# A fused attention and FFN kernel: a planner in the kernel fixes one issue order for all engines, and the opening goes by query tiles

## The chip, the cores and the metric

The kernel runs on one core of a Trainium2 chip. Times are device microseconds (us) of that core, medians over several executions. The "span" is the time from the first to the last instruction of the one execution that the profile shows; the device time is 1.7 to 1.9 us more than the span (2.7 in one run). A core has a matrix engine (TensorE, PE in the profile, with PEld for its weight loads), VectorE (DVE), ScalarE (ACT), GpSimd (POOL) and a sync engine (SP). GpSimd and the sync engine only issue DMAs here, apart from a little set-up. Each engine works through its own list of instructions in order; semaphores make it wait for the others.

## The reference, cut to what matters

```python
# q, k, v: (4 batches, 8 heads, 768 rows, 64) float32
scores = (q @ k.T) / 8 + bias            # bias falls with distance, one slope per head
scores = where(keep, scores, -1e9)       # keep: the last 96 rows, and the first 8 ("global") ones
a = exp(scores - max);  a = a / sum(a)
x = (a @ v) as (3072, 512)               # heads side by side
h = maximum(x @ w_in, 0)                 # w_in  (512, 2048)
out = (h * h) @ w_out                    # w_out (2048, 512)
```

As a row looks back at most 95 rows, a tile of 128 queries needs two blocks of keys: its own tile and the one before ("before" blocks, in which the first rows are replaced by the global ones: `kb` and `vb` are the copies of k and v made so).

## The kernel before

Work goes by eight half batches of 384 rows (three tiles of 128), numbered 0 to 7. While TensorE does the FFN of one half batch, the attention of the next is mixed in. In the names of the profile: `trp` are the transposes of q and k, `sp` the scores, `ex` and `phat` the exponentials and the weighted ones, `av` the product with v, `tm` the normalised result, `trx` its transposes and `xt` the FFN input; `hps`, `hr` and `h` belong to the first FFN layer, `yps` and `y` to the second. Only TensorE's order is fixed by hand; the framework orders the other engines.

```python
def score(b, half, a, g):                # twice per head pair a: g = 0, 1
    ...
    sp = ps_big.tile([P, 2, 512], FP32, name="sp", tag="big")     # 3 buffers of 2 PSUM banks
    for i, (r, before) in enumerate(blocks):                      # 2 or 3 blocks
        for e in range(2):                                        # two heads, 64 rows each
            nc.tensor.matmul(sp[:, e, i * P:(i + 1) * P], lhsT=..., rhs=..., start=True, stop=True)
    nc.scalar.activation(out=ex[:, :, 0:n], in_=sp[:, :, 0:n], func=AF.Exp, scale=scale)
    nc.vector.tensor_tensor(out=phat[:, :, c0:c0 + n], in0=ex[:, :, 0:n], in1=mask[...], op=ALU.mult)

def attention(hb):                       # the list of side jobs
    jobs = [lambda: fix_v(b, half)]      # the vb copies on VectorE
    for a in range(NPAIR + 3):           # prep, score 0, score 1, attend, to_x, staggered
        ...

fill_index()
for h0 in range(0, H, 4):
    load(0, 0, h0, h0 + 4)               # 18 DMAs of four heads each, all on GpSimd
fill_masks()
for c in range(4): load_w_in(c)
load(0, 1, 0, H)
for c in range(4): load_w_out(c)
load(1, 0, 0, H)
with tc.manual_schedule(engines={PE}):
    for job in attention(0): job()
    for hb in range(NHB):
        if 1 <= hb and hb + 2 < NHB: load((hb + 2) // 2, hb % 2, 0, H)
        main = ffn(hb)                   # 16 jobs of the first layer, 12 of the second
        side = attention(hb + 1) if hb + 1 < NHB else []
        for job in merge(main, side, 1, len(main) - 4): job()
```

The softmax here doesn't subtract the row's maximum and nothing guards it: scores larger than these inputs give would overflow.

Of the kernel before, what the change touches and what calls it, by code (L numbers as in the profile page):

```python
# [8 lines left out]
FP32 = mybir.dt.float32  # L9
# [3 lines left out]
PE = mybir.EngineType.PE  # L13

P = 128


def merge(main, side, start, stop):

    out = []  # L20
    done = 0
    for i, f in enumerate(main):
        if i >= start:
            want = len(side) if i >= stop else (i - start) * len(side) // (stop - start)
            while done < want:
                out.append(side[done])
                done += 1
        out.append(f)
    return out + side[done:]
# [3 lines left out]
def kernel(  # L33
# [23 lines left out]
    GR = 32  # L57
    scale = 1.0 / math.sqrt(D)
    slopes = [2.0 ** (-8.0 * (h + 1) / H) for h in range(H)]

# [6 lines left out]
    phat_p = ctx.enter_context(tc.tile_pool(name="phat", bufs=3))  # L67
    tm_p = ctx.enter_context(tc.tile_pool(name="tm", bufs=3))
    h_p = ctx.enter_context(tc.tile_pool(name="hp", bufs=2))
    y_p = ctx.enter_context(tc.tile_pool(name="yp", bufs=2))  # L70
    ps_big = ctx.enter_context(tc.tile_pool(name="ps_big", bufs=3, space=bass.MemoryType.PSUM))
    ps_att = ctx.enter_context(tc.tile_pool(name="ps_att", bufs=2, space=bass.MemoryType.PSUM))


    dist = const.tile([P, 2 * P], FP32, name="dist")
    distc = const.tile([P, 2 * P], FP32, name="distc")
    pidx = const.tile([P, 1], FP32, name="pidx")
    ident = const.tile([P, P], FP16, name="ident")
    local = const.tile([P, 2 * P], FP16, name="local")
    ge0 = const.tile([P, 2 * P], FP16, name="ge0")  # L80
    isg = const.tile([P, 1], FP32, name="isg")
    far = const.tile([P, 2 * P], FP16, name="far")
    decay = const.tile([P, H, 2 * P], FP16, name="decay")
    gw = const.tile([P, H, 2 * P], FP16, name="gw")
    cg = const.tile([P, H], FP16, name="cg")

    mask = const.tile([P, H, 5 * P], FP16, name="mask")
# [3 lines left out]
    def fill_index():  # L91
        nc.gpsimd.iota(dist, pattern=[[1, 2 * P]], base=0, channel_multiplier=-1,
                       allow_small_or_imprecise_dtypes=True)
        nc.gpsimd.iota(pidx, pattern=[[0, 1]], base=0, channel_multiplier=1,
                       allow_small_or_imprecise_dtypes=True)
        nc.vector.tensor_scalar(out=ident, in0=dist[:, 0:P], scalar1=0.0, scalar2=None,
                                op0=ALU.is_equal)

    def fill_masks():
        nc.vector.tensor_scalar(out=distc, in0=dist, scalar1=0.0, scalar2=None, op0=ALU.max)  # L100
        for h in range(H):
            nc.scalar.activation(out=decay[:, h, :], in_=distc, func=AF.Exp, scale=-slopes[h])
            nc.vector.memset(cg[:, h:h + 1], math.exp(-slopes[h] * NL))
        nc.vector.tensor_scalar(out=ge0, in0=dist, scalar1=0.0, scalar2=None, op0=ALU.is_ge)
        nc.vector.scalar_tensor_tensor(out=local, in0=dist, scalar=float(NL), in1=ge0,
                                       op0=ALU.is_lt, op1=ALU.mult)
        nc.vector.tensor_scalar(out=isg, in0=pidx, scalar1=float(NG), scalar2=None,
                                op0=ALU.is_lt)
        nc.vector.tensor_scalar(out=far, in0=local, scalar1=0.5, scalar2=isg,
                                op0=ALU.is_lt, op1=ALU.mult)  # L110
        nc.vector.tensor_tensor(out=gw, in0=far[:, None, :].to_broadcast([P, H, 2 * P]),
                                in1=cg[:, :, None].to_broadcast([P, H, 2 * P]), op=ALU.mult)
        own, bef = slice(0, P), slice(P, 2 * P)
        nc.vector.tensor_tensor(out=mask[:, :, P:3 * P], in0=decay,
                                in1=local[:, None, :].to_broadcast([P, H, 2 * P]), op=ALU.mult)
        nc.vector.tensor_tensor(out=mask[:, :, 0:P], in0=mask[:, :, P:2 * P],
                                in1=gw[:, :, own], op=ALU.add)
        nc.vector.tensor_tensor(out=mask[:, :, 2 * P:3 * P], in0=mask[:, :, 2 * P:3 * P],
                                in1=gw[:, :, bef], op=ALU.add)
        nc.vector.tensor_copy(out=mask[:, :, 3 * P:5 * P], in_=mask[:, :, P:3 * P])  # L120


# [3 lines left out]
    batches = []  # L126
    for b in range(B):
        bt = Batch()
        bt.sq = [None, None]
        bt.sk = [None, None]  # L130
        batches.append(bt)

    def load(b, half, h0, h1):
        bt = batches[b]
        if half == 0 and h0 == 0:
            bt.qk = qk_p.tile([P, 2, NPAIR, S], FP16, name="qk", tag="qk")
            bt.kb = qk_p.tile([P, NPAIR, NT - 1, P], FP16, name="kb", tag="kb")
            bt.v = qk_p.tile([P, NT, H, D + 1], FP16, name="v", tag="v")
            bt.vb = qk_p.tile([P, NT - 1, H, D + 1], FP16, name="vb", tag="vb")
            nc.vector.memset(bt.v[:, :, :, D:D + 1], 1.0)  # L140
        if h0 == 0:
            bt.sq[half] = stage_p.tile([P, HT, H, D], FP16, name="sq", tag="sq")
            bt.sk[half] = stage_p.tile([P, HT, H, D], FP16, name="sk", tag="sk")
        rows = slice(half * HALF, (half + 1) * HALF)
        for src, dst in ((q, bt.sq[half]), (k, bt.sk[half]),
                         (v, bt.v[:, half * HT:(half + 1) * HT, :, 0:D])):
            for t in range(HT):
                r0 = half * HALF + t * P
                nc.gpsimd.dma_start(  # L149
                    out=dst[:, t, h0:h1, :],  # L150
                    in_=src[b, h0:h1, r0:r0 + P, :].rearrange("h p d -> p h d"))

    def fix_v(b, half):
        bt = batches[b]
        t0, t1 = (0, HT) if half == 0 else (HT, NT - 1)
        nc.vector.tensor_copy(out=bt.vb[GR:GR * 2, t0:t1], in_=bt.v[GR:GR * 2, t0:t1])
        nc.vector.tensor_copy(out=bt.vb[2 * GR:P, t0:t1], in_=bt.v[2 * GR:P, t0:t1])  # L157
        for t in range(t0, t1):
            nc.vector.tensor_copy(out=bt.vb[0:GR, t], in_=bt.v[0:GR, 0])

    def prep(b, half, a):
        bt = batches[b]
        trp = ps_att.tile([P, 2, HT, P], FP16, name="trp", tag="att")
        for i, st in enumerate((bt.sq[half], bt.sk[half])):
            for t in range(HT):
                nc.tensor.transpose(out=trp[:, i, t, :], in_=st[:, t, 2 * a:2 * a + 2, :],  # L166
                                    identity=ident)
        nc.scalar.copy(out=bt.qk[:, :, a, half * HALF:(half + 1) * HALF],  # L168
                       in_=trp.rearrange("p i t c -> p i (t c)"))
        kt = bt.qk[:, 1, a, :].rearrange("p (t c) -> p t c", c=P)  # L170
        t0, t1 = (0, HT) if half == 0 else (HT, NT - 1)
        nc.vector.tensor_copy(out=bt.kb[:, a, t0:t1, GR:P], in_=kt[:, t0:t1, GR:P])  # L172
        nc.vector.tensor_copy(out=bt.kb[:, a, t0:t1, 0:GR],  # L173
                              in_=kt[:, 0:1, 0:GR].to_broadcast([P, t1 - t0, GR]))


    GROUPS = {
        0: ([(0, 0), (1, 0), (1, 1)], [(2, 0), (2, 1)]),
        1: ([(3, 0), (3, 1), (4, 0)], [(4, 1), (5, 0), (5, 1)]),
    }  # L180
    MASK0 = {0: (0, 1), 1: (1, 2)}
    phats = {}
    tms = {}
    xts = {}

    def score(b, half, a, g):
        bt = batches[b]
        if g == 0:
            phats[b, half, a] = phat_p.tile([P, 2, 6 * P], FP16, name="phat", tag="phat")
        phat = phats[b, half, a]  # L190
        blocks = GROUPS[half][g]
        n = len(blocks) * P
        c0 = 3 * P * g
        m0 = MASK0[half][g] * P
        sp = ps_big.tile([P, 2, 512], FP32, name="sp", tag="big")
        for i, (r, before) in enumerate(blocks):
            for e in range(2):
                rows = slice(e * D, (e + 1) * D)
                lhsT = (bt.kb[rows, a, r - 1, :] if before
                        else bt.qk[rows, 1, a, r * P:(r + 1) * P])  # L200
                nc.tensor.matmul(sp[:, e, i * P:(i + 1) * P], lhsT=lhsT,  # L201
                                 rhs=bt.qk[rows, 0, a, r * P:(r + 1) * P],
                                 start=True, stop=True)
        ex = phat_p.tile([P, 2, 3 * P], FP16, name="ex", tag="ex")
        nc.scalar.activation(out=ex[:, :, 0:n], in_=sp[:, :, 0:n], func=AF.Exp, scale=scale)  # L205
        nc.vector.tensor_tensor(out=phat[:, :, c0:c0 + n], in0=ex[:, :, 0:n],  # L206
                                in1=mask[:, 2 * a:2 * a + 2, m0:m0 + n], op=ALU.mult)
# [161 lines left out]
```

## Time and profile before

The time before was 261.35 us as the median of three runs (261.56 with a fourth).

| TensorE, kernel before | us |
|---|---|
| first FFN matmul | 27.0 |
| first layers of half batches 1 to 7 begin | 67.15, 94.43, 121.96, 151.53, 179.05, 206.06, 233.58 |
| last matmul ends / span | 254.5 / 258.2 |

The head of the page, and the rows for TensorE and its clock in 40 equal slices of the span (6.5 us each; a digit is tenths):

```profile
span 258.2 us, 4590 instructions
...
PE 227.6 (88%) x1888; PEld 125.0 (48%) x1888; DVE 139.6 (54%) x331; ACT 135.0 (52%) x201; POOL 75.9 (29%) x95
...
PEclk9999999985999999999999999999999999999999
```

TensorE is busy most of the time, but its clock falls in the ninth and tenth slice (52 to 65 us). The timeline of TensorE shows why. Columns: start in us, us, engine, line, operation, output and inputs, shape, count, and in brackets the idle time before it with what ended it.

```profile
32.94 0.23 PE L166 MATMUL trp<-ident,sk 128*128 128x128 f16 x1 [0.65 <-DMA sk<-in_k_dram]
33.84 0.23 PE L166 MATMUL trp<-ident,sk 128*128 128x128 f16 x1 [0.67 <-DMA sk<-in_k_dram]
...
35.76 0.81 PE L272 MATMUL hps<-xt,w_in_sb 128*128 128x384 f16 x4
36.50 0.23 PE L201 MATMUL sp<-qk 64*128 64x128 f16 x2
36.57 0.22 PE L201 MATMUL sp<-qk,kb 64*128 64x128 f16 x2
36.62 0.22 PE L201 MATMUL sp<-qk 64*128 64x128 f16 x2
36.77 0.82 PE L272 MATMUL hps<-xt,w_in_sb 128*128 128x384 f16 x4
...
59.26 0.24 PE L220 MATMUL av<-v,phat 128*128 128x65 f16 x1 [5.71 <-DVE tm L227]
...
59.92 1.90 PE L284 MATMUL yps<-w_out_sb,h_389 128*128 128x512 f16 x4
...
126.92 0.81 PE L272 MATMUL hps<-xt,w_in_sb 128*128 128x384 f16 x4 [1.87 <-DVE y L289]
```

At 33 us transposes wait for one key tile after another, 0.9 us apart. At 36.5 us one of the two score groups of a head pair passes: three pairs of matmuls 0.06 us apart, but 0.37 us in all between the FFN matmuls on both sides. At 59.26 us a gap of 5.7 us ends, and the four second-layer matmuls after it take 1.9 us. VectorE's timeline has the cause of the gap:

```profile
54.00 1.76 DVE L159 COPY vb<-v 32x520 f16<-32x520 f16 x5 [5.49 <-DMA v<-in_v_dram]
...
58.65 0.56 DVE L227 TENSOR_TENSOR tm<-av,rec 128x384 f16<-128x384 f32 x1
```

VectorE stood for 5.5 us in front of copies of v that had not landed, and the normalisation `tm` that TensorE needed was behind them. The 1.87 us at 126.92 us are of the same kind: the `y` copy that ended the wait stood behind v copies for which VectorE had waited 2.23 us.

### The profile page before, as it was taken

The numbers are of one execution on the slowest core, as the hardware profiler recorded it, in microseconds if no ns is written. First come the engines' busy times: TensorE is split into PE (matmuls) and PEld (weight loads), VectorE is DVE, ScalarE is ACT, GpSimd is POOL, SyncE is SP. The second block draws the span as 40 slices with busy tenths as digits, with TensorE's granted clock in tenths as the row PEclk, the third lists the DMA queues.
The fourth block names the chain that finished last, engine by engine and source line by source line (L and its number), as shares of the span: only waits on it lengthen the run. The fifth ranks groups of instructions, "written<-read, shape, count | busy, mean of one in ns | idle before, by whom it ended". The sixth has DMA issues, their size and how long they took to land.

```text
span 258.2 us, 4590 instructions
## 1 busy us (share of the span) xinstructions
PE 227.6 (88%) x1888; PEld 125.0 (48%) x1888; DVE 139.6 (54%) x331; ACT 135.0 (52%) x201; POOL 75.9 (29%) x95
## 2 busy tenths in 40 slices
PE   1428769928999999999699999999999999999994
PEld 0216345514555555645455555655654565555541
DVE  8558237454778336746676436843675346543411
ACT  5436359601297329941587329831984179623600
POOL 8996573696207000528008000700000000000000
PEclk9999999985999999999999999999999999999999
DMA  6999999999909930499909630792100210003003
GB/s 44 87 116 205 169 179 208 156 153 109 209 1 63 62 121 3 29 96 76 169 3 84 41 122 3 50 76 81 43 0 0 85 41 3 0 5 119 0 3 122
DMA packets 82597, 20.22 MB, mean 78 GB/s; under 512 B 75408, under 2 KB 79504, under 8 KB 82576
## 3 DMA queue, kind: packets, MB, share of 16 engines
q0 software_dynamic: 79248, 13.64, 71.0%
q1 hardware_dynamic: 3328, 6.29, 6.6%
q8 instruction: 15, 0.25, 0.4%
q14 instruction: 6, 0.05, 0.1%
HBM read 27.26 MB, written 6.29 MB: 130 GB/s over the span
## 4 chain that ended last, share of the span: by engine, by line
PE 54%; DMA 17%; ACT 11%; POOL 11%; DVE 3%; issue 2%; DVEq 0%; POOLq 0%
PE yps L284 27%; PE hps L272 19%; DMA v<-in_v_dram 8%; POOL v L149 5%; DMA w_out_sb<-in_moe_w_out_dram 5%; DMA w_in_sb<-in_moe_w_in_dram 5%; ACT hr L276 4%; ACT ex L205 4%; PE av L220 3%; ACT qk L168 3%; PE sp L201 3%; POOL sq L149 2%; POOL sk L149 2%; PE trx L239 1%; POOL w_out_sb L310 1%
## 5 line engine op out<-in xcount | busy, mean ns | idle before, releaser
L272 PE MATMUL hps<-xt,w_in_sb 128*128 128x384 f16 x512 | 98.5, 329 | 2.6 <-DVE y L289 1.9
L276 ACT ACTIVATE hr<-hps 128x768 f16<-128x768 f32 x64 | 52.8, 825 | 43.9 <-PE hps L272 43.0
L272 PEld LDWEIGHTS <-w_in_sb 128*128 128x128 f16 x512 | 45.9, 98 | 31.4 <-issue 3.2
L205 ACT ACTIVATE ex<-sp 128x768 f16<-128x768 f32 x64 | 47.8, 779 | 8.9 <-PE sp L201 8.8
L149 POOL DMA_DIRECT2D sq<-in_q_dram x27 | 23.4, 882 | 71.0 <-PE trp L166 70.5
L206 DVE TENSOR_TENSOR phat<-ex,mask 128x768 f16<-128x768 f16 x64 | 33.0, 523 | 20.5 <-ACT ex L205 17.1
L240 ACT COPY xt<-trx 128x384 f16<-128x384 f16 x32 | 15.3, 478 | 41.1 <-PE trx L239 41.1
L168 ACT COPY qk<-trp 128x768 f16<-128x768 f16 x32 | 25.2, 808 | 15.3 <-PE trp L166 15.3
L289 DVE COPY y<-yps 128x1024 f32<-128x1024 f32 (+1 forms) x16 | 15.3, 958 | 26.3 <-PE yps L284 26.2
L149 POOL DMA_DIRECT2D v<-in_v_dram x27 | 23.3, 883 | 16.3 <-DVE rec L225 8.2
L149 POOL DMA_DIRECT2D sk<-in_k_dram x27 | 23.1, 878 | 4.1 <-DMA w_out_sb<-in_moe_w_out_dram 2.0
L220 PEld LDWEIGHTS <-phat 128*128 128x128 f16 x352 | 15.9, 102 | 16.4 <-DVE tm L227 6.2
L220 PE MATMUL av<-v,phat 128*128 128x65 f16 x192 | 16.4, 201 | 6.8 <-DVE tm L227 5.7
L166 PE MATMUL trp<-ident,sq 128*128 128x128 f16 x96 | 12.4, 229 | 7.4 <-DMA sq<-in_q_dram 7.4
L220 PE MATMUL av<-vb,phat 128*128 128x65 f16 x160 | 15.7, 200 | 3.3 <-DVE vb L157 3.3
L227 DVE TENSOR_TENSOR tm<-av,rec 128x384 f16<-128x384 f32 x32 | 17.8, 556 | 0.9
L201 PE MATMUL sp<-qk 64*128 64x128 f16 x192 | 17.7, 231 | 0.3 <-ACT qk L168 0.3
L201 PE MATMUL sp<-qk,kb 64*128 64x128 f16 x160 | 16.4, 227 | 1.7 <-DVE kb L173 1.7
L166 PE MATMUL trp<-ident,sk 128*128 128x128 f16 x96 | 12.4, 229 | 4.3 <-DMA sk<-in_k_dram 4.2
L172 DVE COPY kb<-qk 128x288 f16<-128x288 f16 (+1 forms) x32 | 10.2, 320 | 9.3 <-ACT qk L168 6.9
L201 PEld LDWEIGHTS <-qk 64*128 64x128 f16 x192 | 8.0, 97 | 14.8 <-issue 12.6
L166 PEld LDWEIGHTS <-sq 128*128 128x128 f16 x96 | 8.3, 101 | 12.3 <-DMA sq<-in_q_dram 8.8
(56 smaller groups left out, 246.6 us busy)
## 6 DMA issues: line engine op xcount, KB each, us to landing
out_dram<-y SPq DMA_DIRECT2D x8, 512.0 KB, 2.8
sq<-in_q_dram POOLq DMA_DIRECT2D x21, 128.0 KB, 5.7
sk<-in_k_dram POOLq DMA_DIRECT2D x21, 128.0 KB, 5.3
v<-in_v_dram POOLq DMA_DIRECT2D x21, 128.0 KB, 6.4
w_in_sb<-in_moe_w_in_dram POOLq DMA_DIRECT2D x4, 512.0 KB, 8.6
w_out_sb<-in_moe_w_out_dram POOLq DMA_DIRECT2D x4, 512.0 KB, 10.5
out_dram<-y SPq DMA_DIRECT2D x8, 256.0 KB, 2.0
sq<-in_q_dram POOLq DMA_DIRECT2D x6, 64.0 KB, 3.0
```

Of the source, the lines that this page charges most:

```text
L149: nc.gpsimd.dma_start(out=dst[:, t, h0:h1, :], in_=src[b, h0:h1, r0:r0 + P, :].rearrange("h p d -> p h d"))
L166: nc.tensor.transpose(out=trp[:, i, t, :], in_=st[:, t, 2 * a:2 * a + 2, :], identity=ident)
L168: nc.scalar.copy(out=bt.qk[:, :, a, half * HALF:(half + 1) * HALF], in_=trp.rearrange("p i t c -> p i (t c)"))
L201: nc.tensor.matmul(sp[:, e, i * P:(i + 1) * P], lhsT=lhsT, rhs=bt.qk[rows, 0, a, r * P:(r + 1) * P], start=True, stop=True)
L205: nc.scalar.activation(out=ex[:, :, 0:n], in_=sp[:, :, 0:n], func=AF.Exp, scale=scale)
L206: nc.vector.tensor_tensor(out=phat[:, :, c0:c0 + n], in0=ex[:, :, 0:n], in1=mask[:, 2 * a:2 * a + 2, m0:m0 + n], op=ALU.mult)
L220: nc.tensor.matmul(av[:, e, j, :], lhsT=phat[:, e, i * P:(i + 1) * P], rhs=bt.vb[:, r - 1, h, :] if before else bt.v[:, r, h, :], start=n ...
L227: nc.vector.tensor_tensor(out=tm.rearrange("p t e d -> p e t d"), in0=av[:, :, :, 0:D], in1=rec[:, :, :, None].to_broadcast([P, 2, HT, D]) ...
L240: nc.scalar.copy(out=xts[hb][:, a, :], in_=trp.rearrange("p t c -> p (t c)"))
L272: nc.tensor.matmul(st["ps"][:, m2, 0:HALF], lhsT=w_in_sb[:, kk, m * P:(m + 1) * P], rhs=xt[:, kk, :], start=kk == 0, stop=kk == NCT - 1)
L276: nc.scalar.activation(out=hr, in_=st["ps"][:, :, 0:HALF], func=AF.Relu)
L284: nc.tensor.matmul(st["y"][:, j % 2, :], lhsT=st["h2"][:, m, j * P:(j + 1) * P], rhs=w_out_sb[:, m, :], start=m == 0, stop=m == NFT - 1)
```

## The change

The intent is to shorten the opening and to leave TensorE no gaps. It has these parts.

- A small planner in the kernel lists all operations with guessed costs, simulates the engines greedily (what can start first goes first) and issues everything in the order that it found. Where ScalarE and VectorE can both do a PSUM evacuation, it picks one. TensorE's own order is still a given list.
- The first half batch's attention goes by tiles of 128 queries (T, S, A, X for transposes, scores, attention, transposes back), and its first layer begins on tile 0 (F), then tiles 1 and 2 (G). The first layer of half batch 1 runs before the second layer of half batch 0, so that w_out is needed later.
- The first key tiles come over the sync queue in float32 and are cast. w_in is loaded in two parts, before and after the q, k and v of half batch 1.
- From half batch 2 on, the two score groups of a head pair are issued as one. PSUM is used as six buffers of one bank instead of three of two.
- Smaller parts: the masks are made by ScalarE from a clamped distance instead of by products on VectorE, `kb` and `vb` hold one block less, and some SBUF buffers are more.

```diff
-    with tc.manual_schedule(engines={PE}):
...
+OPENING = """T0 S0o V0 T1 T2 S1o S1b A01 A00 X00 S2b A10 A11 S2o X01 X10 A20 A21 F1 t0 t1 F0 X21 X11 s0o
+X20 s0b t3 t2 G10 s1o s1b V1 G20 a0 G00 G30 x0 s3b s3o a1 s2o G11 s2b F3 a3 x1 F2 G21 a2 G01
+x3 x2 G31"""
...
+    def load(self, dur, emit, needs=(), rank=None):
+        ...
+        op = Op({"POOL": 0.9}, emit, needs, rank, 1.0, land=dur)
...
+    def run(self):
+        ...
+        while self.rest or any(self.queues.values()):
+            ...
+            for op in [q[0] for q in self.queues.values() if q] + self.rest:
+                r = self.ready(op)
+                ...
+                e = min(op.costs, key=lambda e: max(r, self.free.get(e, 0.0)) + op.costs[e])
+                c = (max(r, self.free.get(e, 0.0)), op.rank, e, op)
+                if best is None or c[:2] < best[:2]:
+                    best = c
+            ...
+            if op.land is not None:
+                self.landed = max(end + 0.8, self.landed) + op.land
+                op.done = self.landed + op.lag
...
+            return plan.load(0.62, emit, vbefore if name == "v" else before)
...
+        costs = {"DVE": 0.2 + 0.75 * n, "POOL": 0.6 + 2.1 * n}
+        x.vb_op = plan.add(costs, emit, x.v_in)            # the vb copies
...
+    list_w_in((0, 1))
+    list_loads(x1)
+    list_w_in((2, 3))
+    list_w_out()
...
+    for job in l1(x1) + l2(x0):
+        job()
+    for hb in range(1, NHB):
+        x = halves[hb]
+        if hb + 1 < NHB:
+            list_loads(halves[hb + 1])
+        main = l2(x) if hb == 1 else l1(x) + l2(x)
+        side = attention(halves[hb + 1]) if hb + 1 < NHB else []
+        merge(main, side, 1, len(main) - 1)
+    with tc.manual_schedule():
+        order = plan.run()
```

## The prediction

> **What bounds it now.** TensorE, except early. By the page it is busy 227.6 of 258.2 us. The TensorE timeline shows the half batches starting their first layer at 27.0, 67.15, 94.6, 122.0, 151.5, 179.2, 206.2 and 233.7 us: 27.0 to 27.7 us each from 67 us on (one 29.6: 1.9 us behind the y copies). Of that, 64 first-layer matmuls at 0.163 us and 48 second-layer ones at 0.217 us are 20.8 us; attention about 6.6. Losses: 27 us until the first FFN matmul (attention there is some 6.5 us of warm TensorE work), 40.1 instead of 27.4 us for the first half batch, about 2 us later, 3.7 us of tail. For the extra 12.7 us, the waits show transposes waiting for query and key DMAs (30.7 to 34.7 us, one tile per 0.88 us) and 5.7 us until 59.3, because VectorE, in order, sits behind a v load. After that gap the clock row falls to about 0.5 and four second-layer matmuls take 1.9 us, not 0.87; the Trainium skill, "TensorE: Matmul & The Clock Gate", Part 1, says an idle window lowers the clock, and the trace agrees.
>
> **What changes.**
> 1. Opening. The first half batch's loads are 9 issues instead of 18 (each 0.77 to 0.88 us on GpSimd), key ones on the sync queue. Attention goes by tiles of 128 queries, w_in 0 and 1 come next, first-layer matmuls start on tile 0, and the first layer of half batch 1 runs before the second layer of 0. Estimate from traced rates (0.88 us a q/k/v tile, 2.6 us a weight chunk): first nine tiles by about 10.5 us, w_in 0 and 1 by 16, second q and k by 21, w_in complete by 29, w_out by 40. After 21 us TensorE has some 16.5 us left in the opening list, ScalarE plus VectorE about 33 us between them, so it ends near 38 to 39 us. With the second layer of half batch 0 (10.4 us) that equals what the old kernel has done at 67.15: **17 to 18 us gained**.
> 2. Scores of a head pair are one group, not two. A group of three block pairs takes 0.37 us, of which 0.18 is switching (the Trainium skill, "TensorEngine Tiling (Array Packing)", Key Properties: mode switching drains TensorE). Four saved per half batch, six half batches: **4.4 us gained**.
> 3. VectorE no longer meets v loads late: **about 2 us gained**.
> 4. ScalarE and VectorE work per half batch stays near 35 us in 26.7. But scores take four of six single-bank buffers, and a fixed order passes errors of the plan on (it plans 0.62 us per q/k/v tile; I read 0.88): **1.5 us lost**, above all where attention of half batch 2 is squeezed into one second layer.
>
> All counted is on the critical path: TensorE has nothing else to do in those gaps. 258.2 - 17.5 - 4.4 - 2 + 1.5 = 236 us of span; the time is 3 us more than the span: about 238 us. As the plan may open better than my serial estimate, **237 us, 229 to 246**; faster by over 2% 0.96, same 0.03, slower 0.01.
>
> **What would show it.** First FFN matmul near 16 us; second layer of half batch 0 ending near 59 to 60 us; no idle over 3 us after 25 us, no clock dip at 52 to 64; later half batches 26.5 to 27 us each; TensorE busy about 93%. Wrong if: transposes wait for the second half batch's loads past 23 us; half batches stay at 27.4 or longer because matmuls wait for relu or exp to free a bank; ScalarE, with masks and exponentials, stretches the opening past 42 us; loads on the sync queue (256-byte pieces) land late; VectorE slows while GpSimd makes descriptors.

## The result, and the profile after

The changed kernel took 241.96 us (240.93 to 242.27, four runs) beside 261.56 us before: a ratio of 0.9239 (95% interval 0.9203 to 0.9275). Ratios are the mean time of one kernel's runs over that of the other's in the same rounds, so they are not quite the ratio of the medians quoted. The prediction was 237 us, 229 to 246.

The head of the page and the clock row, after:

```profile
span 240.2 us, 4887 instructions
...
PE 220.5 (92%) x1952; PEld 131.2 (55%) x1952; DVE 126.4 (53%) x341; ACT 147.0 (61%) x334; POOL 67.1 (28%) x83
...
PEclk9999999999999999997999999999999999999999
```

The gap near 59 us and its clock dip are gone. But there is a new dip in the nineteenth slice (108 to 114 us). TensorE's timeline at the points that answer to those before:

```profile
7.18 0.60 PE L550 MATMUL trp<-ident,sq 128*128 128x128 f16 x4 [7.18 <-DMA sq<-in_q_dram]
...
11.55 0.61 PE L550 MATMUL trp<-ident,sq 128*128 128x128 f16 x4 [0.86 <-DMA sq<-in_q_dram]
...
20.74 1.90 PE L471 MATMUL hps<-xt,w_in_sb 128*128 128x128 f16 x16
...
35.45 1.07 PE L471 MATMUL hps<-xt,w_in_sb 128*128 128x128 f16 x16
...
51.62 8.58 PE L519 MATMUL yps<-w_out_sb,h 128*128 128x512 f16 x39
...
103.23 1.03 PE L519 MATMUL yps<-w_out_sb,h 128*128 128x512 f16 x4
106.70 0.34 PE L452 MATMUL trx<-ident,tm 128*128 128x128 f16 x3 [2.45 <-DVE tm L438]
```

The first FFN matmul is at 20.7 us, not 27.0. The second layer of half batch 0 starts at 51.62 us and ends 10.4 us later; as the first layer of half batch 1 is then done too, 51.6 us is what compares with 67.15 before: 15.5 us gained in the opening. From there on only some 2.5 us more were gained.

The clock row hides one thing. The trace has no clock record before 25.4 us, and the row prints 9 there all the same. But the sixteen matmuls at 20.74 us start 0.106 us apart (the next instruction starts at 22.43), and sixteen of the same shape at 35.45 us start 0.056 us apart: TensorE ran at about half rate until some 25 us, in the kernel before until some 29 us. All runs below open like this. By the first clock record of their profiles the half rate ends at 22.5 to 22.8 us in `e1`, `e5` and `e10`, at 23.7 in `e6`, at 28.5 in `e12` and at 31.4 to 32.4 in `e3`, `e7` and `e11`. Where an opening is compared below, this difference is a part of it, and no run was made to separate it.

The new gap is at 104 to 106.7 us, and VectorE has it again:

```profile
99.11 1.01 DVE L406 TENSOR_TENSOR phat<-ex,mask 128x768 f16<-128x768 f16 x2
103.71 2.10 DVE L186 COPY vb<-v 32x1560 f16<-32x1560 f16 x3 [3.58 <-DMA v<-in_v_dram]
105.80 0.24 DVE L436 RECIPROCAL rec<-av 128x6 f32<-128x6 f32 x1
105.93 0.10 DVE L267 MEMSET v<- 128x48 f16 x1
106.09 0.56 DVE L438 TENSOR_TENSOR tm<-av,rec 128x384 f16<-128x384 f32 x1
```

VectorE is done with `phat` at 100.1 us, then stands in front of v copies until 103.7. The reciprocal behind them was ready to run since about 101.5, when TensorE's last `av` matmul of that group ended. What makes it odd: the shape (three tiles, 1560 columns) tells that these are the copies of half batch 5, whose attention begins only at about 135 us. Nobody needed them.

So I printed the times that the planner itself had computed, which is no measurement, but says what it believed. It put v of half batch 5 as landed at 97.4 us of its own clock, 10.5 us after the first of the nine loads began to issue; found VectorE free at 97.5; and set the copies there, ahead of a normalisation at 100.05. On the chip the nine loads began to issue at 90.9 us and v landed at 103.7, 12.8 us later. Even with a delay of 10.5 us the copies would not have fitted well; with 12.8 they stop VectorE and through it TensorE. The plan as a whole promised 229.2 us of span, against 240.2.

Half batches from one first layer to the next show the cost:

| from the first layer of half batch | before | after |
|---|---|---|
| 2 to 3 | 27.5 | 29.5 |
| 3 to 4 | 29.6 | 27.2 |
| 4 to 5 | 27.5 | 27.7 |
| 5 to 6 | 27.0 | 25.95 |
| 6 to 7 | 27.5 | 26.4 |

The undisturbed ones (5 and 6) are 1.1 us shorter than before; those with v copies of half batches 5 and 7 in the way (2 and 4) are not, and 3 runs partly on the lowered clock.

### The profile page after: what moved, and what is told of

Its sections match the earlier page's. It is cut to its first block, busy times and chain, and to the rows that moved or that the text cites. A ratio compares the mean times of both kernels' runs of the same rounds, so it can differ in the third digit from the quotient of the medians.

```text
span 240.2 us, 4887 instructions
## 1 busy us (share of the span) xinstructions
PE 220.5 (92%) x1952; PEld 131.2 (55%) x1952; DVE 126.4 (53%) x341; ACT 147.0 (61%) x334; POOL 67.1 (28%) x83
## 4 chain that ended last, share of the span: by engine, by line
PE 75%; DMA 9%; POOL 9%; DVE 3%; issue 1%; ACT 1%; POOLq 0%; DVEq 0%
PE hps L471 35%; PE yps L519 27%; DMA v<-in_v_dram 5%; DMA sk<-in_k_dram 4%; POOL sq L260 4%; PE sp L375 4%; PE trp L330 4%; PE av L429 3%; POOL sk L260 3%; DVE vb L186 2%; PE trx L452 2%; POOL v L260 1%; DVE tm L438 1%; POOL w_in_sb L296 1%; POOLq L755 0%
## 5 line engine op out<-in xcount | busy, mean ns | idle before, releaser
L471 PE MATMUL hps<-xt,w_in_sb 128*128 128x384 f16 (+2 forms) x576 | 95.5, 316 | 0.0
L519 PE MATMUL yps<-w_out_sb,h 128*128 128x512 f16 x384 | 92.5, 380 | 0.0
L495 ACT ACTIVATE hr<-hps 128x384 f16<-128x384 f32 (+1 forms) x108 | 54.5, 509 | 17.5 <-PE hps L471 14.6
L519 PEld LDWEIGHTS <-h 128*128 128x128 f16 x384 | 34.8, 98 | 33.7
L506 DVE TENSOR_TENSOR h<-hr 128x768 f16<-128x768 f16 (+1 forms) x68 | 35.1, 529 | 34.3 <-ACT hr L495 33.6
L390 ACT ACTIVATE ex<-sp 128x384 f16<-128x384 f32 x112 | 44.4, 498 | 1.1 <-PE sp L375 1.1
L184 ACT COPY xt<-trx 128x384 f16<-128x384 f16 (+1 forms) x32 | 14.7, 464 | 31.4 <-PE trx L452 31.4
L184 ACT COPY y<-yps 128x512 f32<-128x512 f32 x23 | 13.5, 586 | 28.9 <-PE yps L519 28.5
L184 ACT COPY qk<-trp 128x384 f16<-128x384 f16 (+1 forms) x39 | 18.0, 498 | 5.8 <-PE trp L330 3.1
L406 DVE TENSOR_TENSOR phat<-ex,mask 128x768 f16<-128x768 f16 x32 | 16.5, 550 | 0.4 <-ACT ex L390 0.4
L436 DVE RECIPROCAL rec<-av 128x6 f32<-128x6 f32 x28 | 5.4, 194 | 20.6 <-PE av L429 20.6
```

The source lines that it names most:

```text
L184: nc.scalar.copy(out=out, in_=in_)
L390: nc.scalar.activation(out=st["ex", g][:, h, 0:n], in_=st[g][h][:, 0:n], func=AF.Exp, scale=scale)
L406: eng(e).tensor_tensor(out=phat[:, :, c0:c0 + n].rearrange("p e (i c) -> p e i c", c=P), in0=ex[:, :, 0:n].rearrange("p e (i c) -> p e i c ...
L471: nc.tensor.matmul(st["ps"][:, i * n:(i + 1) * n], lhsT=w_in_sb[:, kk, m * P:(m + 1) * P], rhs=x.xt[:, kk, c0:c1], start=kk == 0, stop=kk ...
L495: nc.scalar.activation(out=o, in_=i, func=AF.Relu)
L506: eng(e).tensor_tensor(out=x.h2[:, m0:m0 + width, c0:c1], in0=hr, in1=hr, op=ALU.mult)
```

## The experiments

Theory A: the changed kernel falls short because VectorE, in order, is put in front of v copies too early, by a planner that thinks loads land sooner than they do. Its rival B: VectorE or the loads are the limit there in any case. The other runs measure the parts of the change one at a time. All runs gave correct results; most are compared with the run `e5_gate_exact` or with the changed kernel, at 241.96 us and 241.11 in its second visit (`e9`).

### 1. The v copies may not be planned early

```diff
-        x.vb_op = plan.add(costs, emit, x.v_in)
+        x.vb_op = plan.add(costs, emit, x.v_in + x.turned[:1])   # and listed after the first turn()
```

> Only the place of the v copies (the ones that build vb) in VectorE's order changes: they may be planned only after the first transposes of their own half batch. Theory A: the TensorE idle time near 104 to 107 us and near 161 us, and the clock dip after the first, come from VectorE standing behind v copies of a half batch that is not needed for another 25 us, because the plan holds v to have landed earlier than it does. Then both gaps and the dip vanish: 237 us, 4 to 6 us less than the changed kernel. Rival B: the v data or VectorE itself is the limit there, and the wait only moves to another instruction: within 1.5 us of the changed kernel's 242 us.

Measured: 235.44 us (235.34 to 236.32), ratio 0.9052. Theory A holds. As this edit also moved one TensorE job by a slot, it was repeated with TensorE's order untouched:

```diff
-        x.vb_op = plan.add(costs, emit, x.v_in)
+        x.vb_op = plan.add(costs, emit, x.v_in + (halves[x.hb - 1].attended[-1:] if x.hb > 1 else []))
```

> Like the first run, but with TensorE's order left exactly as in the changed kernel: the v copies of a half batch may be planned only after the last attention matmuls of the half batch before. Theory A (VectorE's order was the cause): as fast as the first run, 234 to 237 us, both gaps gone, half batches from 77 us on 26 to 26.5 us each. Rival B (the shift of one TensorE job in the first run was the gain): 240 to 242 us.

Measured: 236.08 us (235.34 to 236.55), ratio 0.9068. VectorE and then TensorE in the same stretch of this run:

```profile
101.25 0.26 DVE L436 RECIPROCAL rec<-av 128x6 f32<-128x6 f32 x1 [1.43 <-PE av L429]
101.40 0.10 DVE L267 MEMSET v<- 128x48 f16 x1
101.56 0.56 DVE L438 TENSOR_TENSOR tm<-av,rec 128x384 f16<-128x384 f32 x1
```

```profile
102.92 1.03 PE L519 MATMUL yps<-w_out_sb,h 128*128 128x512 f16 x4
103.78 0.33 PE L452 MATMUL trx<-ident,tm 128*128 128x128 f16 x3
103.95 1.03 PE L519 MATMUL yps<-w_out_sb,h 128*128 128x512 f16 x4
104.81 3.41 PE L471 MATMUL hps<-xt,w_in_sb 128*128 128x384 f16 x20
```

The normalisation now waits for TensorE's matmuls, not for v, and the transposes follow without a gap. The clock row is 9 throughout after the opening, and the half batches from 2 on take 26.4, 25.95, 26.4, 25.95 and 26.4 us. So the early v copies cost about 5 us (241.1 to 242.0 against 236.1 by the medians, 4.1 to 4.5 by the ratios). The changed kernel's trace has them as 3.5 us of gaps (2.45 and 1.07) and some 1.7 us lost to the clock after the first.

### 2. Only the planner's figures for a load

```diff
-        op = Op({"POOL": 0.9}, emit, needs, rank, 1.0, land=dur)
+        op = Op({"POOL": 0.9}, emit, needs, rank, 2.0 if dur < 1 else 1.0, land=dur)
...
-            return plan.load(0.62, emit, vbefore if name == "v" else before)
+            return plan.load(0.95, emit, vbefore if name == "v" else before)
```

> No gate on the v copies; only the planner's figures for a load change, to what the trace shows (0.95 us a tile and 2 us to landing, instead of 0.62 and 1). Theory A: the early v copies are a consequence of the plan's optimistic landing times, so a truer figure alone moves them behind the last normalisation of the half batch before, and the gaps go: 235 to 238 us. Rival B: the greedy planner puts copies of far-off data early in any case, and the gaps stay: 240 us or more.

Measured: 236.39 us (236.0 to 237.28), ratio 0.9083. The changed kernel on the same chip:

> The changed kernel once more, on the same chip as the next three, for a ratio without a change of chip: 240.5 to 242.5 us, ratio 0.924; both idle gaps near 106 and 162 us again.

241.11 us (238.51 to 242.13), ratio 0.9226, with both gaps again in its profile (the profiled run, 242.13, is over 1.5% above the fastest; its clock, 0.993, is that of the changed kernel's other runs. The fastest, at 238.51, kept the full clock). VectorE with the truer figures:

```profile
101.82 0.56 DVE L438 TENSOR_TENSOR tm<-av,rec 128x384 f16<-128x384 f32 x1
103.72 2.10 DVE L186 COPY vb<-v 32x1560 f16<-32x1560 f16 x3 [1.33 <-DMA v<-in_v_dram]
```

The copies still start the moment v lands, but behind the normalisation, and nobody waits. Theory A holds here too: the origin of this loss is two numbers in the plan, and here truer ones are enough. That they would be enough in another kernel is not shown: the planner still starts the copies as soon as it holds v to have landed.

### 3. Scores in two groups again

```diff
-                jobs.append(lambda a=a - 1: score(x, a))
+                jobs.append(lambda a=a - 1: score(x, a, 0))
+                jobs.append(lambda a=a - 1: score(x, a, 1))
```

On the changed kernel as it is:

> From half batch 2 on, the scores of a head pair are issued as two groups again with other matmuls between (24 groups more). Theory A: each costs 0.18 us of switching on TensorE, which is the bound: 4.4 us longer. Rival B: the gain of the later half batches comes from other things (finer PSUM buffers, balanced evacuation), and the two groups cost under 1.5 us.

Measured: 242.52 us (the four fast runs 241.89 to 243.22), ratio 0.9323, which is 0.6 to 1.4 us over the changed kernel's two medians, or 2.2 us by the ratios. Inconclusive. So it was repeated on the gated kernel:

> The scores in two groups again, on top of the run before, where no idle gap blurs it. Theory A: 24 groups at 0.18 us on the bound engine: 4.4 us longer than the run without, and each half batch that holds attention 0.7 to 0.9 us longer. Rival B: under 2.5 us, as the same test without the v copies' fix seemed to say.

Measured: 240.4 us (239.92 to 240.63), ratio 0.9235: 4.3 us longer, as predicted. From the first layer of half batch 5 to that of 6 it took 26.8 us instead of 25.95. One of the second groups, in TensorE's timeline:

```profile
171.82 0.49 PE L471 MATMUL hps<-xt,w_in_sb 128*128 128x384 f16 x2
172.24 0.34 PE L375 MATMUL sp<-qk 64*128 64x128 f16 x6
172.52 0.82 PE L471 MATMUL hps<-xt,w_in_sb 128*128 128x384 f16 x4
```

Why did the first of the two runs show less? Not because its half batches were cheaper: 5 to 6 and 6 to 7 took 26.8 and 27.3 us in its profile, 0.85 us more than in the changed kernel, as in the second run. The record offers another reason. The changed kernel's clock was lowered after its gap (0.978 to 0.993 in seven of eight runs), while this run, with a gap of 2.31 us in the same place, kept 0.997 to 1.000 and so did not pay those 1.7 us. Against the one changed run at full clock, 238.51 us, its fast runs are 3.4 to 4.7 us longer. That is a single run, so this is likely and not shown. The lesson of the pair: measure a cost on TensorE where neither gaps nor the clock differ.

### 4. The opening by head pairs

On the gated kernel (the gate of `e5` is in the edit too):

```diff
-    for name in OPENING.split():
-        jobs[name]()
+    for job in attention(x0):
+        job()
+    merge(l1(x0), attention(x1), 1, NFT - 1)
```

> The opening by head pairs with whole half batches, as in the kernel before, with everything else of the change (loads, planner, first layer of half batch 1 before the second of 0). Theory A: going by query tiles is worth what it lets start before the second half batch's data is there: 5 to 8 us (the plan says 7.3). Rival B: the loads' order and the planner make the opening, and tiles give less than 3 us.

Measured: 242.76 us (241.95 to 244.23), ratio 0.9334: 6.7 us longer. But not all of that is the tiles. In this run TensorE and VectorE met once more like this (TensorE first, then VectorE):

```profile
28.16 0.50 PE L452 MATMUL trx<-ident,tm 128*128 128x128 f16 x3 [3.59 <-DVE tm L438]
```

```profile
25.31 2.10 DVE L186 COPY vb<-v 32x1560 f16<-32x1560 f16 x3 [1.30 <-DMA v<-in_v_dram]
27.34 0.17 DVE L436 RECIPROCAL rec<-av 128x6 f32<-128x6 f32 x1
```

The gate does not cover half batch 1, and its v copies now stop the last normalisation of half batch 0: 3.6 us. Also, TensorE stayed at half rate until 31.8 us, not 22.8. Going by tiles is worth at most 6.7 us here; taking off the wait leaves about 3 us, an estimate, and how much of that is the lower rate stays open.

### 5. Only TensorE's order is fixed

```diff
-    with tc.manual_schedule():
+    with tc.manual_schedule(engines={mybir.EngineType.PE}):
```

> The changed kernel with only TensorE's order fixed; the other engines' orders are left to the framework, as in the kernel before. Theory A: the planner's order of the other engines is worth little by itself, as it also holds the error with the v copies: within 3 us of the changed kernel's 242 us, perhaps faster. Rival B: the fixed order of all engines is the main gain: 248 us or more.

Measured: 252.61 us (251.72 to 253.72), ratio 0.9708: 10.6 us longer than the changed kernel. My theory A was wrong, rival B holds. Who waited for whom (us in total, times, longest):

```profile
PE trp L550 <- DVE ident L207: 8.7, 1, 8.7
PE trx L452 <- DVE tm L438: 6.4, 2, 6.1
PE sp L577 <- DVE qk L186: 4.6, 2, 3.2
PE sp L375 <- DVE qk L186: 1.9, 1, 1.9
```

With the framework's order the very first transposes wait until 8.7 us for the identity matrix, because VectorE has casts of late key loads in front of it, and near 50 us TensorE waits 6.1 us for a normalisation that has v copies in front of it. Around the wait near 50 us, and again from 125 us on, the clock was at 0.5 for 6.8 us, where the changed kernel has one stretch of 3.4 us. So without the fixed order of the other engines more than half of the change's gain is lost, errors and all; part of the loss is this lower clock.

### 6. The loads of the opening

All of w_in before the second half batch's loads:

```diff
-    list_w_in((0, 1))
+    list_w_in((0, 1, 2, 3))
     list_loads(x1)
-    list_w_in((2, 3))
```

> All four parts of w_in are loaded before the second half batch's q, k and v (undoes the two parts). Theory A: the second half batch's first transposes wait until about 27.5 us instead of 22.4, TensorE has nothing else in its fixed order, and the time grows by 4 to 6 us. Rival B: ScalarE and VectorE bound the opening from 20 to 40 us anyway, and the time grows by less than 2 us.

Measured: 245.73 us (244.91 to 246.18), ratio 0.9436: 4 to 5 us longer. The transposes of half batch 1 wait for their loads one by one, from 23.55 to 28.02 us, where those of the changed kernel start at 22.43; the second layer of half batch 0 starts at 57.3 us instead of 51.6. Theory A holds. In its profile the run gets 2.8 us of these 5.7 back: half batches 2 and 3 take 27.8 and 25.95 us instead of 29.5 and 27.2, as its waits behind v copies are shorter (1.3 us at most) and leave the clock alone.

The first half batch's keys on GpSimd in 16 bit, without casts:

```diff
+        if x.hb == 0:
+            ...
+            for t in range(HT):
+                x.q_in.append(rows(q, "sq", t)); x.k_in.append(rows(k, "sk", t)); x.v_in.append(rows(v, "v", t))
```

> The keys of the first half batch go over the GpSimd queue in 16 bit, as all others, instead of the sync queue in 32 bit with casts. Theory A: the sync loads share the DMA engines with the first query tile, which took 5.8 us from issue to landing where the kernel before took 2.8; without them the first transposes start near 6 us instead of 7.2, the third tile is no earlier, and the time stays within 1.5 us. Rival B, what the plan in the kernel computes: nine serial issues on GpSimd push everything back and the time is 4.5 us longer.

Measured: 243.58 us (243.4 to 245.96), ratio 0.9378: 1.6 to 3.6 us longer than the changed kernel, between the theories. The lines of TensorE's waits in this run:

```profile
PE trp L556 <- DMA sq<-in_q_dram: 6.3, 2, 5.2
...
PE trx L647 <- DVE tm L633: 4.5, 1, 4.5
```

The first query tile is there at 5.2 us instead of 7.2 (3.8 us from issue to use instead of 5.8), so the sync loads did slow it. That agrees with the Trainium skill, "DMA: Bandwidth & Descriptors", Issuing engines are not separate DMA queues: all queues run on the same DMA engines. But the gain is lost, as TensorE then waits 4.5 us for a normalisation.

The first half batch's query tiles before its v tiles (with the gate):

```diff
-                x.v_in.append(rows(v, "v", t))        # in the loop, after each query tile
+            x.v_in += [rows(v, "v", t) for t in range(HT)]   # after the loop
```

> With the gate; the first half batch's three query tiles are loaded before its three v tiles instead of in turn. Theory A: the third transposes start near 9 us instead of 11.5, ScalarE's exponentials start earlier, and the first FFN matmul comes 1 to 2 us earlier; but the second half batch's keys land no earlier, so the time changes by under 1.5 us against the gated kernel's 236. Rival B: what the plan computes, 3.5 us longer, because v is then late for the first attention matmuls.

Measured: 239.2 us (238.49 to 240.1), ratio 0.9181: 3.1 us longer than with the gate alone. My theory A was wrong: the third transposes did start earlier (10.25 us instead of 11.55), but the first FFN matmul stayed at 20.67. The plan computed 3.5 us for it, though it was not v for the first attention matmuls. VectorE's timeline, then TensorE's:

```profile
26.14 2.10 DVE L186 COPY vb<-v 32x1560 f16<-32x1560 f16 x3 [4.50 <-DMA v<-in_v_dram]
28.17 0.40 DVE L506 TENSOR_TENSOR h<-hr 128x512 f16<-128x512 f16 x1
28.50 0.58 DVE L186 COPY kb<-qk 128x288 f16<-128x288 f16 x4
```

```profile
24.73 1.91 PE L471 MATMUL hps<-xt,w_in_sb 128*128 128x128 f16 x16
...
28.89 0.50 PE L375 MATMUL sp<-qk,kb 64*128 64x128 f16 x6 [0.93 <-DVE kb L186]
```

The first of these lines in the gated kernel:

```profile
24.38 1.06 PE L471 MATMUL hps<-xt,w_in_sb 128*128 128x128 f16 x16
```

The order for VectorE came out differently, and VectorE now stands 4.5 us in front of the v copies of half batch 1, with key copies behind them that TensorE waits for. In the gated kernel the same key copies run at 25.4 us, before the v copies. It is the same picture again, but TensorE's wait for these copies is only 0.93 us of the 3.8 by which the second layer of half batch 0 starts later (55.09 us instead of 51.33). Sixteen first-layer matmuls took 1.7 us to the next start where the gated kernel's took 0.9: TensorE was at half rate until 32.4 us instead of 22.8. Whether the stop on VectorE kept the rate down, no run shows.

Only one part of w_in before the second half batch's loads, the opening list permuted to match (with the gate):

```diff
-    list_w_in((0, 1))
+    list_w_in((0,))
     list_loads(x1)
-    list_w_in((2, 3))
+    list_w_in((1, 2, 3))
... OPENING: F0 in the place of F1, F1 and G2, G3 later
```

> With the gate; only one part of w_in is loaded before the second half batch's q, k and v, and the opening list is permuted to match (F0 for F1, and F1, G2, G3 later). Theory A: the second half batch's landing limits the opening, its first transposes start near 21 us instead of 23 and the second layer of half batch 0 at 49.5 to 50.5 instead of 51: 1 to 2 us shorter than the gated kernel, about 234.5 us. Rival B: what the plan computes, 2.3 us longer, because ScalarE and VectorE bound the stretch and w_in parts come late.

Measured: 236.44 us (236.3 to 237.28), ratio 0.9087: no gain, against 236.08. My theory fell. The transposes no longer wait for loads, but they start at 22.28 us all the same, because the attention of half batch 0 on TensorE lasts until 20.6 and the first sixteen FFN matmuls, before them in the list, until 22.28; and the second layer starts at 52.5 us, not 50. In the gated kernel, between 30 and 42 us ScalarE is busy 10.7 and VectorE 10.5 of 12 us. That speaks for these two as the bound there, but TensorE is shown busy for nearly all of the same 12 us, and in this run it was at half rate until 28.5 us instead of 22.8. No run tested which of the three it is.

### What beats both kernels

The three kernels with the v copies out of the way (235.44, 236.08 and 236.39 us) beat the kernel before and the changed one. They don't differ beyond noise.

## Why the prediction was right or wrong

The prediction held: 241.96 us lies in 229 to 246, and the gain of 19.6 us is 80% of the 24.4 forecast. Its parts fared differently, and that the sum came out within 5 us is in part luck: the parts that were too hopeful (about 2 us in the opening, about 4 on errors of the plan) were offset by some 1.5 us of gain that nobody had forecast or explained.

- **Opening, 17 to 18 us gained: right in kind, 2 us too much.** Measured 15.5 us (51.6 against 67.15). The term that was mis-sized is the first FFN matmul, "near 16 us": it came at 20.7. I let the arrival of w_in set it and did not cost the chain of half batch 0's attention, which takes 13.5 us from its first transposes at 7.2 us, the first query tile itself being later than I thought. The opening list ended at about 41 us instead of 38 to 39. Part of that chain is TensorE at half rate: it is busy for 9.4 of the 13.6 us up to the first FFN matmul, some 4.7 us more than at full rate (an estimate: half of 9.4). Which link of the chain is the tightest stays open: earlier query tiles alone did not move its end, and no run changed the rate.
- **Scores in one group, 4.4 us: right.** 4.3 us where TensorE is the bound, with 24 groups, hence 0.18 us for each pair of switches. The Trainium skill, "TensorEngine Tiling (Array Packing)", Key Properties, says that a change of tiling mode drains TensorE; the runs give the size of the cost, but do not show that draining is what it consists of.
- **"VectorE no longer meets v loads late", 2 us gained: wrong, and the step that failed.** The one wait that the 2 us stood for (1.87 us, at 126.9 us before) did go. But the same meeting was moved to other places, 104 and 161 us, and cost about 5 us. In the sum it is the prediction's fourth point that was mis-sized, a fixed order that passes errors of the plan on: 1.5 us for that and PSUM together, against about 5. I took "all loads are planned" to mean "none is met late". What I had not asked is what a greedy planner does with work that is not urgent: it starts it as soon as it thinks that it can, in front of urgent work. I had even read that the plan's 0.62 us per tile was too short (0.88 in the trace), but drew only a vague loss from it. Gate and load figures each took the loss away.
- **The other half of that 1.5 us, too few PSUM buffers: not seen.** In TensorE's waits of the changed kernel no FFN matmul waits for a relu or an exponential. Without the v copies the later half batches take 25.95 to 26.4 us, even below my 26.5 to 27.
- **No idle over 3 us after 25 us, no clock dip at 52 to 64: held.** The dip came elsewhere, after the new gap of 2.45 us. The Trainium skill, "TensorE: Matmul & The Clock Gate", Part 1, says that an idle window of about 3.4 us lowers the clock. These traces agree in kind, but not in the length: 2.45 us here and 1.94 us in `e8` were followed by a clock of 0.5, while 2.43 us in `e2` and 2.31 us in the slow run of `e4`, at the same place in the program as the 2.45, were not. So gaps of this length lower the clock in some executions and not in others. Here 20 first-layer matmuls after the gap took 4.5 us, where 3.25 is usual, and four second-layer ones before them 1.3 instead of 0.86: the gap cost some 1.7 us more than its own length.

The balance of the span: 15.5 us in the opening, and from there to the end 8 us with the gate (4.3 of them the scores, about 2 the wait that the kernel before had at 125 us; some 1.5 us were not traced to a cause) less about 5.5 us that the v copies took, clock included, is 18 us: 258.2 to 240.2.

## What to carry to other kernels

In a fixed order for engines that run in order, an early start is not free: a copy that nobody needs yet blocks all behind it when its data is late, so give prefetch-like work a lower bound in the plan, or be pessimistic about landing times. Check a plan against the trace operation by operation; two wrong load figures cost about 5 us here, while giving up the planned order cost over 10. Measure the cost of an instruction on the bound engine only in a kernel where that engine really is the bound. And compare the spacing of matmuls of one shape before you compare two openings: it shows the rate of TensorE even where the clock row has no record.

## What the Trainium skill lacked or had wrong

- "TensorEngine Tiling (Array Packing)" says that a mode switch drains TensorE, but has no figure: 24 more groups of 64-row matmuls between full-size ones cost 4.3 us, 0.18 us for going there and back.
- "DMA: Bandwidth & Descriptors", Anatomy of one DMA — SWDGE, fits one load as 2.0 us plus bytes over 436 GB/s, from which one estimates 2.6 us for a q, k or v tile (256 KB read). Such loads, nine to a half batch and cast to 16 bit in pieces of 64 values, took 5.3 to 6.5 us each from issue to landing (medians of the changed kernel's page), one per 0.88 us; the page has no figure for a backlog of casting loads.
- "TensorE: Matmul & The Clock Gate" names the queues of ScalarE and VectorE as strictly first in, first out, which the traces confirm (a ready reciprocal stood 4.3 us behind a v copy); no page draws from it that an early prefetch copy on VectorE can stop TensorE. Nor does it say what one gap shorter than its window does to the clock; the four lengths above are what these runs show.
